# Chunked attention and a gated feed-forward block: a written table of the operations' order in place of a scheduler run at build time, and a third slot for keys

## The chip, the cores and the metric

The kernel runs on one core of a Trainium2 chip. The metric is the device time of one execution in microseconds (us); lower is better.

## What is computed

Four sequences of 768 positions go through attention with 8 heads of 64, and then through a feed-forward block (512 to 1024 and back) with a gate. All is float32; the block's weights come as float64 words. The reference, cut to its core:

```python
for c in range(S // 32):                        # 24 chunks of queries
    l, r = max(0, 32*c - 16), min(S, 32*c + 40) # keys: 16 to the left, 8 to the right
    k_full = concat([mem_k, k[:, :, l:r]])      # and 8 memory keys; v_full likewise
    scores = (q[:, :, 32*c:32*c+32] @ k_full.T) / sqrt(64)
    out[:, :, 32*c:32*c+32] = softmax(scores) @ v_full
x = out as (4, 768, 512)
h = maximum(x @ w_in, 0)
conv = sum(conv_w[j] * h[:, j-1 shifted] for j in 0..2)   # along the positions
result = (h * sigmoid(conv)) @ w_out
```

## The kernel before, in words

The attention is cut into 32 operations, numbered n = 0 to 31: four for each half of a batch's positions (two heads each). Each loads a query tile (384 KB), a key tile (252 KB) and a value tile (384 KB), and then goes through scores (TensorE, L526, 24 matmuls in the 64-row tiled form), their maximum (L535), exponential, sum and division on VectorE, ScalarE and GpSimd (L540 to L572), a transposition, the product with the values (L632, 24 tiled matmuls), and a split of the result into a high and a low part (L635, L638), because the feed-forward products are made of three matmuls each, high by high, high by low and low by high. The transposition goes one of two ways, by the letter in `TURN`: "P" is three matmuls on TensorE (L585) and two copies on ScalarE (L592); "B" is a VectorE transpose (L603), a store to DRAM (L610) and two loads back (L615).

The feed-forward block works by batch: for each of eight slices of 128 hidden features and each half of the positions four steps of three matmuls (L655), then a ReLU; then the gate: a first tap on ScalarE (L681) or VectorE (L685), two more on VectorE (L690), the sigmoid (L693), the product of gate and h on VectorE or GpSimd (L697, letter in `MULT`), and a split into high and low (L702, L705, letter in `LO`). The second product (L718) has six tiles of 128 positions for each batch, eight steps of three matmuls each, a copy (L730) and a store (L734). Weights come in 16 pieces of 512 KB; `from_f64` makes a high and a low part of each, in one of several ways by the letters in `W_IN` and `W_OUT` (R and S with GpSimd's help, M on VectorE, C with ScalarE and GpSimd; a small letter puts one more instruction on GpSimd).

Nothing is issued as the program text stands. Every operation is first put into a `Plan`, with its engine, an assumed cost, a due time out of the table `DUE`, and the tiles it reads and writes; a tile belongs to a pool of slots (`u` 32, `w` 8, `k` 2, `w64` 4 and others). `Plan.run` then plays a simulated timeline, always issues the operation that can start first, by due time among equals, gives tiles their slots, and so fixes the order of the instructions on each engine and in SyncE's queue, through which all DMAs go. On the chip each engine and the queue work in that order, with semaphores between them; a load whose slot isn't free yet holds up every DMA behind it in the queue.

Of the kernel before, what the change touches and what calls it, by code (L numbers as in the profile page):

```python
# [21 lines left out]
NG = NC // 4  # L22
# [7 lines left out]
W_IN, W_OUT, W_CONV = "RMRRCSmr", "MMsScMRC", "M"  # L30
TAP = "AAAAAAVAAVAAAAAAAAVAAVAAAVVAVVAA"
MULT = "VVVGGGVVVGVVGGGGVVGVVGVGGVVGVVVV"
LO = "GVGVVVGGGVVVVVVGGVVVVGVGVGGGGVGG"
SOFT = "VVVVAVAVVVVVVAVAAVAAVVVVAAVAAVVV"
NORM = "GGVVGVGVVGGVGVVGVVVGVGGGVVVGGVGG"
KEEP = "KKKKKNNKKKKKKKKKNKKNNKKNKKNKKNNN"
TURN = "PPPPPPPPBPPBBBBPBBBBPBBBBBBBBBBP"

NU, NW, NK, NE, NA, N64, ND = 32, 8, 2, 3, 2, 4, 4

DUE = {
    "s": [
        -1747.4, -1723.11, -1347.22, -2305.8, -515.97, -91.42, -519.99, -74.77, -3.93, -23.08, 192.31, 394.01, 594.69,
        739.5, 627.96, 843.01, 980.41, 1080.29, 1036.96, 1102.97, 1195.06, 1154.32, 1725.81, 1459.86, 1808.08, 1825.19,
        2056.74, 2405.75, 3024.16, 4272.87, 4420.77, 5096.5,
    ],
    "x": [
        91.99, -984.01, 194.09, 284.75, 339.58, 92.3, 474.48, 424.73, 617.31, 732.06, 742.88, 570.24, 740.55, 840.07,
        827.86, 798.03, 1011.48, 1314.01, 881.59, 1429.56, 1647.93, 1828.11, 1861.16, 1847.69, 1461.7, 1929.84, 2133.48,
        3255.82, 4126.36, 2450.86, 3882.79, 4443.02,  # L50
    ],
    "z": [
        -497.25, -1022.37, -802.58, -289.23, -254.62, -1989.87, -103.33, -205.74, 288.57, -38.79, 65.72, -185.05, 538.06,
        626.96, 491.31, 95.49, 812.34, 1202.49, 806.09, 775.96, 1402.03, 493.56, 2113.26, 1301.38, 1166.49, 986.07, 5915.43,
        5883.56, 6010.45, 4393.97, 4802.83, 4849.77,
    ],
    "t": [
        403.22, 353.24, 332.59, 206.21, -905.28, 65.06, 534.99, 549.9, 636.01, 49.69, 400.09, 693.94, 550.92, 538.53,
        817.29, -606.94, 1153.58, 1304.96, 1055.69, 1495.28, 928.66, 1223.65, 1604.09, 1933.16, 2927.48, 2953.06, 1576.53,
        1798.48, 3734.97, 3794.57, 3033.27, 474.2,  # L60
    ],
    "p": [
        -1059.09, -645.56, -1491.31, -515.31, -415.67, -370.98, -140.64, 75.41, 192.02, 185.23, 433.84, -1978.48, 1014.73,
        818.34, 1439.11, 913.87, 1051.08, 995.86, 2163.84, 1264.46, 2048.92, 3116.62, 1998.39, 3357.56, 4793.09, 4879.62,
        5091.42, 5234.16, 5814.05, 3832.44, 3305.69, 5616.03,
    ],
    "b": [
        1312.85, 933.59, 2887.81, 2282, 2349.62, -94.87, -335.28, 131.64, 364.48, 4687.61, 404.65, 402.37, 633.73, 488.76,
        947.78, 1079.68, 1364.67, 1388.86, 1126.48, 1474.55, 2587.02, 2225.91, 2240.2, 2275.95, 3047.5, 2282.08, 3131.22,
        4577.91, 4647.89, 3535.82, 4762.4, 4239.27,  # L70
    ],
    "v": [
        -1982.49, -1932.67, 479.47, 2099.28, -381.54, 965.03, 1258.45, 1250.02, -432.28, -1997.79, -75.7, -2213.02, -1631,
        -2645.37, 986.28, 303.05, 412.98, -1904.27, -1882.24, 2067.69, 2187.15, -661.87, -294.37, 1472.37, 994.33, 1203.8,
        156.84, 1188.6, 1838.38, 2565.39, 914.94, 1193.87,
    ],
    "y": [
        686.52, 535.63, -757.65, 213.4, -1131.77, 3664.3, 1180.6, 1187.05, -1996.08, -2069.13, -2391.68, -2255.33, 2252.87,
        2426.18, 2577.94, 1767.37, 2904.92, 268.81, 740.16, 1370.82, 3119.59, 4087.13, 1289.4, -2124.16, 1248.74, 1110.03,
        1261.16, -2264.79, 1018.78, -1817, 1016.52, -1388.46,  # L80
    ],
    "rt": [
        -1339.84, -1295.03, -1210.04, -1161.56, -1063.49, -177.47, 139.89, 230.96, 672.21, 615.52, 786.3, 834.64, -1154.66,
        417.82, 1248.11, 1230.62, 1355.39, 689.91, 1375.92, 1505.3, 1500.35, 1002.59, 1206.38, 1555.86, 1459.78, 398.77,
        389.95, 108.41, 927.28, 4860.95, 971.48, 4419.35,
    ],
    "ra": [
        -1586.58, -1104.67, -1041.09, -453.16, 117.35, -211.33, 212.08, 400.73, 726.13, 738.27, 457.13, 809.63, 898.1,
        967.26, 1085.69, 1239.43, 1248.14, 1233.78, 1319.34, 1383.33, 1597.97, 1679.03, 1957.13, 1876.57, 2224.33, 2130.08,
        2332.43, 2747.52, 3912.08, 3522.04, 4787.82, 4516.19,  # L90
    ],
    "lqk": [
        -2184.6, -1037.97, -1000.09, -680.53, -139.13, 73.02, 9.72, 175.02, 258.51, 342.33, 449.15, 439.23, 466.03, 491.4,
        545.13, 557.81, 552.07, 861.22, 717.22, 715.38, 1018.29, 958.68, 1171, 1221.92, 1665.34, 1562.88, 2097.11, 2021.43,
        2134.67, 2357.47, 2162.54, 2666.46,
    ],
    "lv": [
        -405, -703.08, -137.92, -291.15, 263.38, -552.48, -43.43, 410.07, 488.26, 420.11, 499.94, 90.47, 329.01, 690.21,
        724.31, 834.94, 878.3, 921.12, 936.89, 1051.99, 1375.12, 1236.9, 1356.07, 1509.97, 2132.94, 1944.15, 2135.58,
        2125.46, 3089.84, 3488.81, 4358.76, 2957.63,  # L100
    ],
# [6 lines left out]
    ],  # L108
    "ie": [
        105.95, 80.37, -13.89, -54.84, -45.59, -62.67, -107.56, -422.53,  # L110
    ],
    "gate": [
        -10.06, 2306.12, 5455.64, 5546.3, 158.99, 87.7, 1943.75, 1265.91, 1243.7, -452.88, -451.4, -54.24, -87.23, 118.85,
        -111.53, 553.42, 2290.11, -1048.39, 636.65, 531.99, 5015.97, 1531.62, 774.64, 69.66, 1868.09, 1198.4, 5259.66,
        885.34, 2417.49, 2125.3, 1868.5, 383.67,
    ],
    "split": [
        -355.58, -406.33, 3625.04, 679.92, 2594.31, 1824.34, 1652.02, 1654.83, 1888.18, 1132.05, -930.3, 1494.36, 2476.58,
        2202.13, 2602.5, 2706, 2712.83, 1677.79, 2754.72, -288.56, 1962.08, 1890.86, 2314.55, 3843.58, 1376.46, 1681.41,
        1387.06, 3909.1, 1846.4, 2902.43, 1768.28, 2587.34,  # L120
    ],
    "out": [
        1863.21, 1377.79, 2057.4, 1214.28, 1650.53, 2020.46, 3647.4, 2153.83, 4216.03, 3201.8, 4228.87, 4287.47, 4393.4,
        4637, 4588.06, 5409.11, 5397.43, 3850.7, 7778.7, 4801.5, 5550.03, 5548.13, 6410.98, 6455.76,
    ],
    "os": [
        113.08, 152.59, 297.73, 105.3, 90.85, 113.99, -208.31, 155.03, 465.83, 433.18, 174.61, 290.41, 562.87, 319.82,
        430.89, 424.06, 421.99, 719.96, 269.33, 1108.12, 397.72, 748.36, 448.96, 3168.08,
    ],
    "ux": [  # L130
        553.64, 555.79, 372.67, 300.19, 395.15, 317.35, -2521.52, 117.95, 176.19, -298.7, 891.09, 384.34, 1075.63, -234.06,
        318.46, 37.52, -21.55, -6.71, 1098.98, 1151.73, 1294.63, 835.63, 1393.5, 1169.49, 1945.66, 2128.89, 2160.19,
        1903.78, 2471.98, 1644.84, 2560.1, 2496.61,
    ],
# [712 lines left out]
```

## Time and profile before

| | |
|---|---|
| median of 3 runs | 365.48 us (365.38 to 366.71) |
| profiled execution | 368.8 us, of which the span from first to last instruction is 367.0 us |
| TensorE busy | 339.7 us (93% of the span), mean granted clock 0.981 |
| VectorE busy | 247.8 us (68%) |
| ScalarE, GpSimd busy | 209.3 us (57%), 112.7 us (31%) |
| DMA | 56.08 MB |

In the views PE is TensorE's matmuls and PEld its weight loads, DVE VectorE, ACT ScalarE, POOL GpSimd, SPq SyncE's queue. "<-" in a group stands between what is written and what is read. Idle time is put down to the engine or DMA that ended it.

### The profile page before, as it was taken

The numbers are of one execution on the slowest core, as the hardware profiler recorded it, in microseconds if no ns is written. First come the engines' busy times: TensorE is split into PE (matmuls) and PEld (weight loads), VectorE is DVE, ScalarE is ACT, GpSimd is POOL, SyncE is SP. The second block draws the span as 40 slices with busy tenths as digits, with TensorE's granted clock in tenths as the row PEclk, the third lists the DMA queues.
The fourth block names the chain that finished last, engine by engine and source line by source line (L and its number), as shares of the span: only waits on it lengthen the run. The fifth ranks groups of instructions, "written<-read, shape, count | busy, mean of one in ns | idle before, by whom it ended". The sixth has DMA issues, their size and how long they took to land.

```text
span 367.0 us, 7407 instructions
## 1 busy us (share of the span) xinstructions
PE 339.7 (93%) x2943; PEld 301.2 (82%) x2943; DVE 247.8 (68%) x427; ACT 209.3 (57%) x382; POOL 112.7 (31%) x118
## 2 busy tenths in 40 slices
PE   1599899999998989999999988999999999999996
PEld 1489789989897979988987867988988888888885
DVE  1988799999987998899998988214736886000000
ACT  2567766898875977757769676224636654121011
POOL 2455534323134144473433122100010628320000
PEclk9969999999998998999999999999999999999999
DMA  7999473348888384653043868403000010111021
GB/s 254 408 397 361 156 272 103 107 148 268 284 253 284 95 283 128 187 188 118 0 139 121 274 220 271 141 33 123 3 29 0 30 58 29 59 57 57 29 88 57
DMA packets 28114, 56.08 MB, mean 153 GB/s; under 512 B 3248, under 2 KB 14896, under 8 KB 28080
## 3 DMA queue, kind: packets, MB, share of 16 engines
q1 hardware_dynamic: 28080, 55.61, 45.3%
q8 instruction: 23, 0.38, 0.4%
q14 instruction: 11, 0.09, 0.1%
HBM read 45.57 MB, written 10.03 MB: 151 GB/s over the span
## 4 chain that ended last, share of the span: by engine, by line
PE 50%; DVE 14%; DMA 11%; ACT 4%; issue 3%; SPq 2%; POOL 1%; POOLq 0%; DVEq 0%; ACTq 0%
PE f L718 29%; PE f L655 16%; DVE w L690 6%; DMA w<-in_q_dram 6%; PE s L526 3%; DMA t_dram<-w 2%; DMA a_d<-t_dram 2%; PE ta L632 2%; DVE u L697 1%; SPq L615 1%; DVE z L567 1%; DMA k<-in_k_dram 1%; DVE e L572 1%; DVE w L603 1%; DVE u L638 1%
## 5 line engine op out<-in xcount | busy, mean ns | idle before, releaser
L655 PE MATMUL f<-u,w_in_hi 128*128 128x384 f32 x512 | 141.7, 347 | 0.7 <-DVE u L638 0.7
L718 PE MATMUL f<-w_out_hi,u 128*128 128x512 f32 (+1 forms) x400 | 125.6, 388 | 1.1 <-ACT u L669 1.1
L655 PEld LDWEIGHTS f<-u,w_in_hi 128*128 128x128 f32 x512 | 94.8, 191 | 3.8 <-DVE u L638 2.0
L718 PEld LDWEIGHTS f<-w_out_hi,u 128*128 128x128 f32 x400 | 74.0, 188 | 17.9 <-ACT u L669 1.5
L655 PE MATMUL f<-u,w_in_lo 128*128 128x384 f32 x256 | 87.4, 341 | 0.1
L690 DVE SCALAR_TENSOR_TENSOR w<-u,cw,w 128x768 f32<-128x768 f32 x64 | 73.2, 1166 | 6.3 <-ACT w L681 6.0
L718 PE MATMUL f<-w_out_lo,u 128*128 128x512 f32 (+1 forms) x200 | 77.1, 385 | 0.0
L669 ACT ACTIVATE u<-f 128x384 f32<-128x384 f32 x64 | 30.9, 493 | 36.8 <-PE f L655 27.4
L655 PEld LDWEIGHTS f<-u,w_in_lo 128*128 128x128 f32 x256 | 49.1, 192 | 0.9 <-POOL u L668 0.4
L730 ACT COPY w_top<-f 128x512 f32<-128x512 f32 (+1 forms) x25 | 14.1, 573 | 59.8 <-PE f L718 59.1
L718 PEld LDWEIGHTS f<-w_out_lo,u 128*128 128x128 f32 x200 | 37.6, 188 | 7.5 <-POOL w_out_lo L481 0.4
L632 PE MATMUL ta<-a_d,w 128*64 128x64 f32 x768 | 29.4, 230 | 6.6 <-DMA a_d<-t_dram 3.3
L572 POOL TENSOR_TENSOR e<-e,z 128x384 f32<-128x384 f32 x16 | 16.8, 1047 | 61.2 <-DVE z L569 43.8
L632 PEld LDWEIGHTS ta<-a_d,w 128*64 128x64 f32 x768 | 26.1, 143 | 11.1 <-issue 6.7
L697 POOL TENSOR_TENSOR u<-w,u 128x768 f32<-128x768 f32 x11 | 18.5, 1683 | 52.6 <-ACT w L693 52.6
L693 ACT ACTIVATE w<-w 128x768 f32<-128x768 f32 x32 | 26.7, 845 | 11.3 <-DVE w L690 11.0
L705 POOL TENSOR_TENSOR u<-u,u 128x768 fp32r<-128x768 f32 x9 | 17.9, 1990 | 36.5 <-ACT u L702 36.5
L535 DVE TENSOR_REDUCE top<-s 128x6 f32<-128x384 f32 x32 | 17.4, 546 | 16.2 <-PE s L526 16.0
L526 PEld LDWEIGHTS s<-k,w 128*64 128x64 f32 x672 | 22.6, 142 | 6.7 <-issue 3.5
L526 PE MATMUL s<-k,w 128*64 128x64 f32 x672 | 25.3, 229 | 2.8 <-DMA w<-in_q_dram 1.4
L705 DVE TENSOR_TENSOR u<-u,u 128x768 fp32r<-128x768 f32 x13 | 17.8, 1377 | 13.2 <-ACT u L702 10.5
L681 ACT ACTIVATE w<-u,cw 128x768 f32<-128x768 f32 x24 | 22.3, 936 | 1.4 <-DVE u L705 0.6
(65 smaller groups left out, 373.8 us busy)
## 6 DMA issues: line engine op xcount, KB each, us to landing
w<-in_v_dram SPq DMA_DIRECT2D x32, 384.0 KB, 4.8
w<-in_q_dram SPq DMA_DIRECT2D x28, 384.0 KB, 4.5
k<-in_k_dram SPq DMA_DIRECT2D x28, 252.0 KB, 4.2
out_dram<-w_top SPq DMA_DIRECT2D x23, 256.0 KB, 2.0
w<-in_w_in_dram SPq DMA_DIRECT2D x8, 512.0 KB, 7.3
w<-in_w_out_dram SPq DMA_DIRECT2D x8, 512.0 KB, 4.4
t_dram<-w SPq DMA_DIRECT2D x19, 192.0 KB, 2.2
a_d<-t_dram SPq DMA_DIRECT2D x38, 96.0 KB, 3.5
```

Source lines behind the costliest of these rows:

```text
L526: nc.tensor.matmul(s.t[j * D : (j + 1) * D, o : o + KW], lhsT=q_[:, c], rhs=k_t.t[:, c * STEP : c * STEP + KW], start=True, stop=True,)
L535: lambda: V.tensor_reduce(out=pairs(top.t), in_=s_(), axis=AX.X, op=ALU.max), (s,), (top,),
L572: lambda: (V if norm == "V" else G).tensor_tensor(out=keys(e), in0=keys(e), in1=pairs(z.t).unsqueeze(3).broadcast_to([P, NG, 2, KW]), op=A ...
L632: nc.tensor.matmul(y, lhsT=v_[:, g, u, h], rhs=a_d.t[:, :, o], start=True, stop=True)
L655: nc.tensor.matmul(f.t[:, :TW], lhsT=w_in_p[c][:, fc, cc], rhs=x.t[:, a * TW : (a + 1) * TW], start=(cc == 0 and i == 0), stop=(cc == NCC ...
L669: A.activation(h.t[:, o : o + TW], f.t[:, :TW], AF.Relu)
L681: plan.op("A", act(S, ptr=1), due, lambda: A.activation(c.t, at(0), AF.Copy, scale=w[0]), H, (c,))
L690: lambda j=j: V.scalar_tensor_tensor(out=c.t, in0=at(j), scalar=w[j], in1=c.t, op0=ALU.mult, op1=ALU.add),
L693: plan.op("A", act(S), due, lambda: A.activation(c.t, c.t, AF.Sigmoid), (c,), (c,), table="sigmoid")
L697: lambda: (V if mult == "V" else G).tensor_tensor(out=y_(), in0=c.t, in1=at(1), op=ALU.mult), (c, h), (y,), shared=True,
L705: lambda: (V if lo == "V" else G).tensor_tensor(out=g_lo(), in0=y_(), in1=g_hi().bitcast(F32), op=ALU.subtract),
L718: nc.tensor.matmul(ps.t[:, :n], lhsT=gs[b, fc][a].t[:, tt * P : (tt + 1) * P], rhs=w_out_p[c][:, fc, o : o + n], start=(fc == 0 and i == 0 ...
```

## The change

`Plan.run` no longer simulates. It walks a table `ORDER` of 1529 numbers, which are the operations' places in the program text, issues them in that order and hands out slots in the order in which they were given back. The table was searched for under transfer times and a clock that were varied. The due times are gone. The key pool gets a third slot; a new table `HOME` puts six of the 32 value tiles into the pool `w64` instead of `w`. The letters are new: thirteen "P" in `TURN` become seventeen, thirteen "G" in `MULT` become twenty-three, and the kinds of the weights change. In the table the first DMA is the first piece of `w_in`; the first query and key tiles follow it.

```diff
-W_IN, W_OUT, W_CONV = "RMRRCSmr", "MMsScMRC", "M"
-MULT = "VVVGGGVVVGVVGGGGVVGVVGVGGVVGVVVV"
-TURN = "PPPPPPPPBPPBBBBPBBBBPBBBBBBBBBBP"
-NU, NW, NK, NE, NA, N64, ND = 32, 8, 2, 3, 2, 4, 4
-DUE = {
...
+W_IN, W_OUT, W_CONV = "SMMSmMCM", "CMMMCMCM", "r"
+MULT = "VGGGGGGVGVGGGGGGVVGVGGGVGVGGVGGG"
+HOME = "wwwwwwwwwwwwwwwwwwwxwwwwwxxxwwxx"
+TURN = "PPPPPPPPBPPBBPBPBPBBPBPBPBBPBBBB"
+NU, NW, NK, NE, NA, N64, ND = 32, 8, 3, 3, 2, 4, 4
+ORDER = [
+    571, 13, 12, 581, 30, 29, 46, 81, 47, 572, 64, 573, 574, 63, 575, 15, 576, 577, 591, 582, 16, 14, 17, 587, 18, 583, 601,
...
     def run(self):
...
+        idle = {k: deque(v) for k, v in self.pools.items()}
+        done = set()
+        for i in ORDER:
+            do, after, tiles = self.ops[i]
+            assert after <= done
             for x in tiles:
                 if x.slot is None:
+                    x.slot = idle[x.pool].popleft()
+                    x.t = x.slot(x.dtype) if callable(x.slot) else x.slot
+            do()
+            done.add(i)
+            for x in tiles:
                 x.left -= 1
                 if not x.left:
+                    idle[x.pool].append(x.slot)
...
-        v_t = Tile("w")
+        v_t = Tile("w" if HOME[n] == "w" else "w64")
+        v_ = lambda: v_t.t if HOME[n] == "w" else v_t.t.rearrange("p n w -> p (n w)")[:, :S].bitcast(F32)
...
-    nc = _bacc.Bacc("TRN2", target_bir_lowering=False, num_devices=1, dynamic_dma_scratch_size=2048)
+    nc = _bacc.Bacc("TRN2", target_bir_lowering=False, num_devices=1, dynamic_dma_scratch_size=1024)
```

The letters of `TAP`, `LO`, `SOFT`, `NORM` and `KEEP` change too; on VectorE they come to two first taps more and one division less, and the small letters to a few GpSimd instructions.

## Rows read from the trace of the kernel before

**Rows 1.** The page, its first two parts: busy time by engine, and VectorE's tenths

```profile
PE 339.7 (93%) x2943; PEld 301.2 (82%) x2943; DVE 247.8 (68%) x427; ACT 209.3 (57%) x382; POOL 112.7 (31%) x118
DVE  1988799999987998899998988214736886000000
```

**Rows 2.** Busy time in four stages: length, five engines with instructions, granted clock, DMA share, GB/s

```profile
0.00:9.18 9.18, 1.55 (x24) 1.39 (x24) 1.34 (x3) 2.73 (x4) 2.26 (x14) 1.00 0.77 254
0.00:170.00 170.00, 149.71 (x1712) 138.02 (x1712) 146.98 (x299) 120.64 (x232) 67.98 (x85) 0.96 0.69 232
170.00:229.00 59.00, 55.35 (x483) 47.48 (x484) 54.80 (x79) 42.64 (x77) 20.43 (x14) 1.00 0.50 160
229.00:363.40 134.40, 134.40 (x750) 115.66 (x748) 46.00 (x51) 45.33 (x73) 24.25 (x20) 1.00 0.15 52
```

**Rows 3.** TensorE's timeline: start, length, instructions, and in brackets what it idled for

```profile
4.56 1.55 PE L526 MATMUL s<-u,u 128*64 128x64 f32 x24 [4.56 <-DMA u<-in_k_dram]
112.07 0.92 PE L632 MATMUL ta<-a_d,w 128*64 128x64 f32 x24 [1.44 <-DMA w<-in_v_dram]
136.92 0.92 PE L632 MATMUL ta<-a_d,w 128*64 128x64 f32 x24 [1.72 <-DMA a_d<-t_dram]
170.02 0.62 PE L655 MATMUL f<-u,w_in_hi 128*128 128x384 f32 x2 [0.28 <-DVE u L638]
215.31 0.92 PE L632 MATMUL ta<-a_d,w 128*64 128x64 f32 x24 [1.25 <-DMA a_d<-t_dram]
225.37 0.92 PE L526 MATMUL s<-k,w 128*64 128x64 f32 x24 [0.79 <-DMA w<-in_q_dram]
```

**Rows 4.** VectorE's timeline, the idle stretches that the text speaks of

```profile
6.14 0.56 DVE L535 TENSOR_REDUCE top<-s 128x6 f32<-128x384 f32 x1 [6.14 <-PE s L526]
114.61 0.56 DVE L535 TENSOR_REDUCE top<-s 128x6 f32<-128x384 f32 x1 [1.53 <-PE s L526]
144.64 0.56 DVE L535 TENSOR_REDUCE top<-s 128x6 f32<-128x384 f32 x1 [0.98 <-PE s L526]
```

**Rows 5.** The chain that ended last, in order of time: start, length, engine, tile, line

```profile
226.29 0.70 PE ta L632 x24
236.96 4.20 PE f L655 x24
249.68 0.89 PE f L718 x3
252.69 0.33 PE ta L585 x3
277.80 85.50 PE f L718 x390
```

**Rows 6.** Groups by line: count | busy us, mean ns | idle before them

```profile
L421 ACT ACTIVATE w_top<-w 128x512 f32<-128x512 f32 (+1 forms) x17 | 11.1, 652 | 11.4 <-DMA w<-in_w_in_dram 5.7 <-DMA w<-in_w_out_dram 5.5
L690 DVE SCALAR_TENSOR_TENSOR w<-u,cw,w 128x768 f32<-128x768 f32 x64 | 73.2, 1166 | 6.3 <-ACT w L681 6.0
L446 DVE TENSOR_SCALAR w<-w 128x512 uint32<-128x512 uint32 (+1 forms) x9 | 3.8, 437 | 0.5 <-DMA w<-in_w_out_dram 0.5
L451 DVE SCALAR_TENSOR_TENSOR w<-w 128x512 uint32<-128x512 uint32 (+1 forms) x9 | 5.6, 629 | 0.0
L603 DVE STREAM_TRANSPOSE w<-e 128x384 f32<-128x384 f32 x19 | 10.5, 564 | 0.1
```

**Rows 7.** Line 697 alone: duration ns min/median/max, first and last start

```profile
L697 POOL TENSOR_TENSOR u<-w,u x11: 1545/1547/2196, 67.4 to 298.8; 128x768 f32<-128x768 f32 x11
L697 DVE TENSOR_TENSOR u<-w,u x11: 945/948/2096, 67.7 to 302.5; 128x768 f32<-128x768 f32 x11
```

**Rows 8.** Line 690 alone, the same columns

```profile
L690 DVE SCALAR_TENSOR_TENSOR w<-u,cw,w x64: 976/1011/2630, 62.3 to 299.4; 128x768 f32<-128x768 f32 x64
```

**Rows 9.** DMA issues by line: count, KB each, median us to landing

```profile
w<-in_v_dram SPq DMA_DIRECT2D x32, 384.0 KB, 4.8
```

**Rows 10.** SyncE's queue: what its DMA issues waited for (us in total, times, longest)

```profile
SPq L406 <- PE s L526: 33.6, 18, 6.3
```

More of the change, by code (lines that the diff above doesn't have):

```diff
@@ L1 @@
-from collections import defaultdict
+from collections import defaultdict, deque
 from contextlib import ExitStack
@@ L182, in pool, with op @@
         self.pools[name] = slots
-    def op(self, eng, cost, due, do, r=(), w=(), shared=False, table=None, mode=None, late=70, gap=380, less=None):
+    def op(self, eng, cost, do, r=(), w=(), shared=False, table=None, mode=None, late=70, gap=380, less=None):
         after = set()
@@ L206, in op @@
             x.left += 1
-            x.due = due if x.due is None else x.due
-        less = LESS.get(eng, 0) if less is None else less
-        self.ops.append((eng, cost, due, do, after - {i}, tiles, shared, table, mode, late, gap, less))
-        return i
+        self.ops.append((do, after - {i}, tiles))
     def over(self, k):
@@ L219, in run @@
     def run(self):
-        ops = self.ops
-        n = len(ops)
-        users = [[] for _ in range(n)]
-        need = [0] * n
-        for i, o in enumerate(ops):
-            need[i] = len(o[4])
-            for a in o[4]:
-                users[a].append(i)
-        ready = [0.0] * n
-        cand = defaultdict(list)
-        for i in range(n):
-            if not need[i]:
-                cand[ops[i][0]].append(i)
-        free, shared_free, queue_free = defaultdict(float, DMA=FIRST), 0.0, 0.0
@@ L302, in run @@
+        assert sorted(ORDER) == list(range(len(self.ops)))
+        idle = {k: deque(v) for k, v in self.pools.items()}
[3 more added lines that the diff above has]
+            assert after <= done
             for x in tiles:
                 if x.slot is None:
-                    x.slot = min(idle[x.pool])
-                    idle[x.pool].remove(x.slot)
-                    x.slot = x.slot[1]
-                    slot = self.pools[x.pool][x.slot]
@@ L308, in run @@
-                    x.t = slot(x.dtype) if callable(slot) else slot
-                    queue[x.pool].remove(x)
+                    x.slot = idle[x.pool].popleft()
[3 more added lines that the diff above has]
+            for x in tiles:
                 x.left -= 1
-                last_use[x] = max(last_use.get(x, 0), end + late)
                 if not x.left:
-                    idle[x.pool].append((last_use[x] + 70, x.slot))
@@ L314, in run @@
-            do()
-            self.times.append((t, end, e, i))
-            for u in users[i]:
-                ready[u] = max(ready[u], end + (late if ops[u][0] != e or e == "DMA" else 0) + (WAIT if ops[u][0] == "DMA" != e else 0))
-                need[u] -= 1
-                if not need[u]:
-                    cand[ops[u][0]].append(u)
-        return max(x[1] for x in self.times)
-CHANGE = {(None, "whole"): 0, (None, "tiled"): 0, ("whole", "tiled"): 95, ("tiled", "whole"): 245}
-FIRST, BEGIN, LAND, WARM = 720.0, 900.0, 1400.0, 3400.0
+                    idle[x.pool].append(x.slot)
@@ L405, in load, with from_f64 @@
             size *= x
-        plan.op("DMA", size * 4 / RATE, due, lambda: nc.sync.dma_start(out=dst(), in_=src), w=w)
-    def from_f64(src, hi, lo, key, n, kind, due, first):
+        plan.op("DMA", size * 4 / RATE, lambda: nc.sync.dma_start(out=dst(), in_=src), w=w)
+    def from_f64(src, hi, lo, key, n, kind):
         w = Tile("w64")
@@ L585, in turn @@
                     nc.tensor.transpose(out=t.t[:, g * P : (g + 1) * P], in_=e.t[:, g, 1 : 2 * KW + 1], identity=ident)
-            plan.op("PE", 327, turn_due, turn, (e,), (t,), mode="whole", late=250)
+            plan.op("PE", 327, turn, (e,), (t,), mode="whole", late=250)
             for p in range(2):
@@ L595, in place @@
                     )
-                plan.op("A", 480, place_due, place, (t,), ((a_d, p),), less=-10)
+                plan.op("A", 480, place, (t,), ((a_d, p),), less=-10)
         else:
@@ L631, in values @@
                             o, y = h * 6 + 2 * g + u, a.t[r, g * P : (g + 1) * P].rearrange("p (j u q) -> p u j q", j=2, u=2)[:, u]
-                        nc.tensor.matmul(y, lhsT=v_[:, g, u, h], rhs=a_d.t[:, :, o], start=True, stop=True)
-        plan.op("PE", 700, sum_due, values, (v_t, (a_d, 0), (a_d, 1)), (a,), mode="tiled", late=250)
-        plan.op("A", act(TW, True), due, lambda: A.copy(out=x.t[:, :TW], in_=a.t[:, :TW]), (a,), ((x, 0),))
+                        nc.tensor.matmul(y, lhsT=v_g[:, g, u, h], rhs=a_d.t[:, :, o], start=True, stop=True)
+        plan.op("PE", 700, values, (v_t, (a_d, 0), (a_d, 1)), (a,), mode="tiled", late=250)
+        plan.op("A", act(TW, True), lambda: A.copy(out=x.t[:, :TW], in_=a.t[:, :TW]), (a,), ((x, 0),))
         plan.op(
-            "V", vec(TW), due,
+            "V", vec(TW),
             lambda: V.tensor_tensor(
@@ L709, in ffn_out @@
     def ffn_out(b, tt, parts=1):
-        start, each = DUE["out"][6 * b + tt], DUE["os"][6 * b + tt]
         n = DM // parts
@@ L732, in ffn_out @@
             plan.op(
-                "DMA", P * n * 4 / RATE, last,
+                "DMA", P * n * 4 / RATE,
                 lambda o_sb=o_sb, o=o: nc.sync.dma_start(
```

292 lines of the change are left out of this document (51 added, 241 removed), and 73 rows, old and new, of tables (DUE, ORDER).

## The prediction

> **What bounds the kernel now.** I read the page first. TensorE is busy 93% of the span, so only about 27 us of its idle time can be won, and VectorE, at 68% on the whole, shows eights and nines from the second slice to the twenty-third and almost nothing in the last five [rows 1]. The busy time by stage makes two halves of that. Up to 229 us both engines are nearly full; from 229 to 363.4 us TensorE is busy for 134.40 of 134.40 us at full clock while VectorE works for 46.0 us [rows 2]. So the last stage is TensorE's alone, no order can shorten it, and the question is when TensorE gets clear of VectorE. TensorE's timeline shows where it stood still before: 4.56 us for the first keys, then 1.44 us for values, 1.72 and 1.25 us for the probabilities' way through DRAM, 0.79 us for a query load, and at 170.02 us it stood once for a VectorE result [rows 3]. VectorE began only at 6.14 us, behind the first scores, and stood 1.53 and 0.98 us for scores that TensorE gave late, each behind one of TensorE's two long DMA waits [rows 3, 4]. Up to 170 us VectorE was busy for 146.98 us, so it idled for 23.0 us, 7.84 of them in the first 9.18 us [rows 2].
>
> In short: the end is (VectorE's work ahead of the tightest point) + (VectorE's idle time up to there) + (TensorE's work behind it) + (TensorE's idle time behind it).
>
> **The change part by part.** Prices on TensorE are those of the dense stretches of the chain: 0.70 us for a block of scores or values, 4.20 / 24 x 3 = 0.525 us for a step of the first product, 85.50 us for 390 matmuls (24 of them half as wide), so 0.68 us for a step of the second, 0.33 us for a turn, and about 0.2 us for a change between tiled and whole matmuls (0.89 against 0.68) [rows 5].
>
> *The flags.* Thirteen operations' turns were on TensorE (P) and seventeen will be: +4 x 0.33 = 1.3 us. I counted the changes between tiled and whole in both orders: 52 before, 54 after, +0.4 us. TensorE gets 1.7 us more to do; at least 4 x 0.175 = 0.7 us (a turn moves no fewer columns than one matmul of the first product). Each turn moved also takes one store and two loads off SyncE's queue, twelve DMAs in all. On VectorE ten products of line 697 go to GpSimd: -10 x 0.95 us [rows 7]. The weights' kinds bring fifteen instructions from GpSimd back to it: seven with one input at about 0.44 and eight with two at about 0.63, +8.1 us [rows 6]. Four transposes fewer, -4 x 0.56 = -2.3 us [rows 6], stand against two first taps more at no more than 1.17 each, by the row of line 690. VectorE's total hardly moves (about -1.4 us), and GpSimd and ScalarE, at 31% and 57% [rows 1], have room for theirs. The ten products cost GpSimd 1.55 us each instead of 0.95 [rows 7]; what is late by 0.6 us is the split that follows, and the second product, which needs it, comes long behind.
>
> *Line 697 and the port.* Line 690 takes 1011 ns in the median and 1166 in the mean over 64, line 697 on VectorE 948 ns in the median and 2096 at most [rows 6, 7, 8]; so some of these instructions are held up, by 0.16 us each on average. The ten moved products may so cost VectorE ten times that, 1.6 us, of which the fifteen weight instructions that leave GpSimd give about as much back. I take nothing; the bounds are nothing and a hold of a whole 1.55 us each (a rival below). The Trainium skill ("SBUF — State Buffer", Who interferes with whom) says that a VectorE instruction with two SBUF inputs and a GpSimd instruction that reads SBUF exclude each other for the whole instruction. Taken at its word for each of the ten, moving them off VectorE wins nothing; the maxima of rows 7 and 8 agree with it, the medians show that most instructions meet no such hold.
>
> *The order.* I numbered the operations as the program makes them and walked both orders, adding to each engine's queue the price of each instruction (its group's mean in the view by line; VectorE's scaled by 0.925, since its means overlap and add up to 267.8 us where 247.8 are busy [rows 1]). For each TensorE step this gives the VectorE work that must be over before it, less the TensorE work ahead of it. Before, the largest difference is 17.8 us, at the first product of batch 2, second half (154.3 against 136.6 of 321.8): the place where TensorE stood for VectorE at 170.02 us [rows 3]. As a check: 170.0 + (321.8 - 136.6) + 3.65 us of TensorE's idle time up to 229 [rows 2] = 358.9 where the chain's last matmul ends at 363.3 [rows 5]; the method is 1.2% short, so I use it for differences alone. After, it is 18.1 us at the turn of operation 22 (148.6 against 130.5), and again 17.4 us at that of operation 24 (192.4 against 174.9). The tight point hardly moves: +0.3 us.
>
> *The loads.* What does move is how early the DMAs stand. Between a load and its first use the old order has on average 4.9 us of TensorE work for queries and 11.9 for values, and for five query and five value loads none at all; the new one has 10.4 and 17.1, and beyond the first five operations never under 5.5. From the last load of the DRAM round trip to the values block it has 5.2 us or more where the old one has often 2.6 to 3.6. A value load takes 4.8 us from issue to landing [rows 9]: the old leads are often below that, the new ones above. The third key slot and the six value tiles moved to another pool make room for this: 18 loads waited 33.6 us for scores to give a slot back [rows 10]. What these leads can win is VectorE's 1.53 + 0.98 us ahead of the tight point and TensorE's 1.25 + 0.79 us behind it [rows 3, 4], 4.55 us. TensorE's own 1.44 and 1.72 us are not added, since VectorE was the later one there. I take two thirds, 3.0 us, as some other operand is late next; bounds 0 and 4.55, and beyond that the clock: 0.96 granted on average over 149.71 busy us up to 170 [rows 2] means some 12 us at 1.2 GHz, 6 us lost, a part of it behind TensorE's two long waits.
>
> *The start.* The new order issues the first weight load ahead of the first query and keys. The first pair, 636 KB, let TensorE begin at 4.56 us [rows 3], so 512 KB issued at the same moment land no later; with 0.65 us on ScalarE [rows 6] VectorE can begin near 4.9 (an estimate, from a landing at 4.2) instead of at 6.14 us [rows 4] and has five instructions (some 2.6 us) to do until the first scores come, about 1.5 us later than now. Before, it did 1.34 us of work by 9.18 us [rows 2]; now I expect 3.7, as about 0.6 us stay idle: -2.4 us. Bounds: nothing (the scores' delay eats it) and -2.9 (no idle time behind 4.9).
>
> **Sum:** +1.7 (TensorE) + 0.3 (tight point) - 3.0 (loads) - 2.4 (start) = -3.4 us. The profiled execution took 368.8 us, 1.8 of them outside its span, and would so come to 365.4; it was 3.3 us above the median of the runs, 365.48, from which the same sum gives 362.1 us.
>
> **The rivals.** *The waits only move.* Slots, not issue times, hold the loads, or an operand from ScalarE is late in their place, and the loads win nothing: 365.48 + 2.0 - 2.4 = 365.1 us. For it: VectorE stays full in both orders, and the tight point stays. *The order wins more.* All 4.55 us of waits go, with 3 of the 6 us at half clock, and the start wins 2.9: 365.48 + 2.0 - 4.55 - 3 - 2.9 = 357.0 us. For it speak the leads; against it that VectorE would have to be busy without a break. *SyncE's queue blocks (slower).* The table's order is also the queue's: where a slot comes free late, every load behind it waits, and the queue waited up to 6.3 us for one slot [rows 10]. One such wait that reaches TensorE, with some 2 us at half clock behind it, gives 362.1 + 8.3 = 370.4 us; it decides from a lead that is overrun by more than 5.5 us. Against it speak the longer leads. *The port (slower).* Each moved product holds VectorE for 1.55 us. Six of the ten lie in the first three batches, ahead of the later tight point: 362.1 + 6 x 1.55 = 371.4 us. By the Trainium skill's rule named above it would come to this; against it stand the medians of rows 7 and 8.
>
> **How the numbers follow.** The forecast has 0.47, the waits that only move 0.23, more won 0.12, the queue 0.12, the port 0.06. About 0.5%, 1.8 us, is what a measurement can tell here, so faster ends at 363.7 and slower begins at 367.3. Faster is the forecast and more won, less a little of the forecast's upper edge: 0.58; same 0.24; slower the two last: 0.18. The forecast's own range is 359 to 364; to hold eight in ten it reaches to the greater gain on one side, 355.5, and into the slower cases on the other, 368.0.
>
> **What would show it.** Right: VectorE's first instruction near 4.9 us; over 3 us less VectorE idle time up to 170 us; no TensorE wait for a load over 1 us between 30 and 230 us; TensorE without a break from some 3 us earlier than 229; 51 turn matmuls. Wrong: a new wait of over 2 us on TensorE, for a DMA or a copy; a mean of line 690 well above 1166 ns; SyncE standing at a slot while the next load is already needed.

## The result, and the profile after

The changed kernel takes 367.88 us in the median of 20 executions (366.09 to 370.45), the kernel before 365.59 us beside it (362.76 to 368.36, 20): a ratio of 1.0072, 95% interval 1.0044 to 1.0100. It is 0.7%, some 2.6 us, slower, where 362.1 us and a gain were forecast. The two profiled executions stand the other way round (368.8 us before, 366.92 us after), because the one of before is a long one of its kind and the one of after a short one; so sizes are taken from the medians, and the profiles serve to show where the time lies.

The page of the changed kernel, busy time and VectorE's tenths:

```profile
PE 339.9 (93%) x2955; PEld 301.4 (83%) x2955; DVE 252.0 (69%) x429; ACT 210.6 (58%) x387; POOL 104.6 (29%) x114
...
DVE  4999999999999999998999956230444991320000
```

Busy time in the stages of [rows 2] (length, then PE, PEld, DVE, ACT, POOL, granted clock, DMA):

```profile
0.00:9.18 9.18, 1.69 (x27) 1.56 (x29) 4.05 (x8) 2.61 (x3) 3.53 (x15) 1.00 0.78 296
0.00:170.00 170.00, 149.82 (x1721) 138.04 (x1722) 158.15 (x301) 126.14 (x250) 55.24 (x78) 0.99 0.67 232
170.00:229.00 59.00, 58.56 (x507) 50.78 (x505) 51.74 (x83) 40.07 (x67) 24.97 (x15) 1.00 0.43 141
229.00:361.50 132.50, 131.00 (x726) 112.24 (x727) 42.09 (x46) 43.99 (x70) 24.34 (x22) 1.00 0.14 50
```

VectorE's idle time up to 170 us is 170 - 158.15 = 11.9 us, where it was 23.0 [rows 2]; the forecast counted on at most 4.9 of that (2.4 at the start, 2.5 at the loads). By 9.18 us it has done 4.05 us of work in this execution (1.34 before, 3.7 forecast), and its first instruction starts at 4.96 us (4.9 forecast), in VectorE's timeline:

```profile
4.96 0.43 DVE L280 TENSOR_SCALAR w_top<-w_top 128x512 f32<-128x512 f32 x1 [4.96 <-ACT w_top L276]
```

TensorE's timeline shows what it stood for (four of its idle stretches, in brackets):

```profile
6.14 1.55 PE L381 MATMUL s<-u,u 128*64 128x64 f32 x24 [6.14 <-DMA u<-in_q_dram]
...
147.94 0.55 PE L439 MATMUL ta<-ident,e 128*128 128x128 f32 x3 [2.14 <-DVE e L427]
...
161.32 0.62 PE L508 MATMUL f<-u,w_in_hi 128*128 128x384 f32 x2 [0.80 <-DVE u L492]
...
230.50 0.44 PE L508 MATMUL f<-u,w_in_hi 128*128 128x384 f32 x1 [1.59 <-ACT u L522]
```

No wait for a load is left between 30 and 230 us; those of [rows 3] are gone, as forecast. In their place stand waits for VectorE's results, 2.14 us at the turn of operation 20 and 0.80 us at 161.32 us, just ahead of the turn of operation 22, where the walk had its tight point (18.1 us). TensorE's last break ends at 230.50 us, where the forecast had it without a break from some 3 us ahead of 229. The idle time that the forecast meant to win is gone, and yet TensorE is no further: up to 170 us it has been busy for 149.82 us, as before (149.71, at a granted clock of 0.96 instead of 0.99). VectorE idles 11 us less and is busy 11 us more.

The groups by line, and line 543 alone as in [rows 8], show a part of what it is busy with (L543 is line 690 of before, L550 line 697):

```profile
L543 DVE SCALAR_TENSOR_TENSOR w<-u,cw,w 128x768 f32<-128x768 f32 x64 | 78.1, 1231 | 4.4 <-ACT w L534 3.7
...
L543 DVE SCALAR_TENSOR_TENSOR w<-u,cw,w x64: 979/1014/2601, 58.4 to 299.5; 128x768 f32<-128x768 f32 x64
...
L550 POOL TENSOR_TENSOR u<-w,u 128x768 f32<-128x768 f32 x16 | 28.9, 1810 | 41.5 <-ACT w L546 41.5
...
L550 POOL TENSOR_TENSOR w<-w,u 128x768 f32<-128x768 f32 x7 | 13.4, 1915 | 11.4 <-ACT w L546 10.5 <-POOL u L521 0.9
```

The two taps on VectorE take 1231 ns in the mean, 1166 before [rows 6]; there are 64 in both. Their median is 1014 ns, as good as the 1011 of [rows 8]: most run undisturbed, and some are more than twice as long. VectorE's total rose by 4.2 us, where a fall of 1.4 was counted. A stretch of the two timelines, VectorE first and then GpSimd, shows how:

```profile
123.30 1.01 DVE L543 SCALAR_TENSOR_TENSOR w<-u,cw,w 128x768 f32<-128x768 f32 x1
...
125.10 2.31 DVE L543 SCALAR_TENSOR_TENSOR w<-u,cw,w 128x768 f32<-128x768 f32 x1
...
128.27 3.22 DVE L543 SCALAR_TENSOR_TENSOR w<-u,cw,w 128x768 f32<-128x768 f32 x2
131.41 0.54 DVE L492 TENSOR_TENSOR u<-ta,u 128x384 fp32r<-128x384 f32 x1
...
132.34 3.23 DVE L543 SCALAR_TENSOR_TENSOR w<-u,cw,w 128x768 f32<-128x768 f32 x2
```

```profile
125.05 1.55 POOL L550 TENSOR_TENSOR u<-w,u 128x768 f32<-128x768 f32 x1 [5.15 <-ACT w L546]
128.36 2.31 POOL L550 TENSOR_TENSOR u<-w,u 128x768 f32<-128x768 f32 x1 [1.77 <-ACT w L546]
132.45 2.31 POOL L550 TENSOR_TENSOR u<-w,u 128x768 f32<-128x768 f32 x1 [1.77 <-ACT w L546]
```

The tap at 123.30 us runs alone, 1.01 us. The one at 125.10 us begins just behind a GpSimd product that started at 125.05 and takes 2.31 us. At 128.27 us it is the other way: the product starts 0.09 us behind the first of two taps and is stretched from 1.55 to 2.31 us, and the second tap waits for it, 3.22 us for the two. They run one after the other, on two engines.

### The profile page after: what moved, and what is told of

It is laid out like the page before. It is cut to its first block, busy times and chain, and to the rows that moved or that the text cites. A ratio compares the mean times of both kernels' runs of the same rounds, so it can differ in the third digit from the quotient of the medians.

```text
span 365.1 us, 7418 instructions
## 1 busy us (share of the span) xinstructions
PE 339.9 (93%) x2955; PEld 301.4 (83%) x2955; DVE 252.0 (69%) x429; ACT 210.6 (58%) x387; POOL 104.6 (29%) x114
## 4 chain that ended last, share of the span: by engine, by line
PE 41%; DVE 21%; ACT 5%; issue 2%; DMA 1%; POOL 1%; SPq 0%; DVEq 0%; ACTq 0%; POOLq 0%
PE f L569 29%; PE f L508 10%; DVE w L543 9%; DVE w_top L293 2%; PE ta L486 1%; DVE e L427 1%; DVE z L422 1%; DVE u L492 1%; DVE top L390 1%; DVE u L557 1%; DMA w<-in_q_dram 1%; ACT u L522 1%; ACT e L413 1%; DVE w L457 1%; DVE e L395 1%
## 5 line engine op out<-in xcount | busy, mean ns | idle before, releaser
L508 PE MATMUL f<-u,w_in_hi 128*128 128x384 f32 x512 | 143.8, 347 | 6.2 <-ACT u L522 3.8
L508 PEld LDWEIGHTS f<-u,w_in_hi 128*128 128x128 f32 x512 | 94.6, 190 | 10.4 <-ACT u L522 5.1
L543 DVE SCALAR_TENSOR_TENSOR w<-u,cw,w 128x768 f32<-128x768 f32 x64 | 78.1, 1231 | 4.4 <-ACT w L534 3.7
L550 POOL TENSOR_TENSOR u<-w,u 128x768 f32<-128x768 f32 x16 | 28.9, 1810 | 41.5 <-ACT w L546 41.5
L492 DVE TENSOR_TENSOR u<-ta,u 128x384 fp32r<-128x384 f32 x32 | 17.5, 548 | 12.8 <-ACT u L489 12.7
L557 DVE TENSOR_TENSOR u<-u,u 128x768 fp32r<-128x768 f32 x9 | 9.4, 1058 | 20.7 <-PE f L569 10.0
L557 POOL TENSOR_TENSOR u<-u,u 128x768 fp32r<-128x768 f32 x11 | 21.5, 1955 | 5.4 <-ACT u L554 3.5
## 6 DMA issues: line engine op xcount, KB each, us to landing
k<-in_k_dram SPq DMA_DIRECT2D x28, 252.0 KB, 4.5
```

Source lines behind the costliest of these rows:

```text
L492: lambda: V.tensor_tensor(out=x.t[:, TW:S], in0=a.t[:, :TW], in1=x.t[:, :TW].bitcast(F32), op=ALU.subtract), (a, (x, 0)), ((x, 1),),
L508: nc.tensor.matmul(f.t[:, :TW], lhsT=w_in_p[c][:, fc, cc], rhs=x.t[:, a * TW : (a + 1) * TW], start=(cc == 0 and i == 0), stop=(cc == NCC ...
L543: lambda j=j: V.scalar_tensor_tensor(out=c.t, in0=at(j), scalar=w[j], in1=c.t, op0=ALU.mult, op1=ALU.add),
L550: lambda: (V if mult == "V" else G).tensor_tensor(out=y_(), in0=c.t, in1=at(1), op=ALU.mult), (c, h), (y,), shared=True,
L557: lambda: (V if lo == "V" else G).tensor_tensor(out=g_lo(), in0=y_(), in1=g_hi().bitcast(F32), op=ALU.subtract),
```

## The experiments

Two theories stood against each other. **P**: a product on GpSimd holds up VectorE's instructions with two SBUF inputs, so that the ten moved products freed nothing. **Q**: VectorE pays for the instructions that it is given, and holds are rare. Later **W** (the weight instructions brought to VectorE), **E** and **V** (what the early loads are worth) and **T** (the product is late on the slower engine) were added. Ratios are to the kernel before, run on the same chip, with 95% intervals; it is the ratios that are compared, since the kernel before itself had medians of 365.56 to 366.62 us beside these runs.

**The old order in a table.** The walker, `ORDER` taken from the old planner, old letters and slots.

> The kernel before with its own order, letters and slots counts, but issued from a table by the new walker (slots handed out in the order of their return). Both theories: the order on each engine is that of before, so 365.6 us within 1 us; if it is slower by over 1 us, the handing out of slots costs something by itself.

Measured 365.91 us, ratio 1.0013 (0.9981 to 1.0045): no change from the walker itself. Its profiled execution (span 364.6 us) had the full clock, and its page serves as a second one of before, here with the busy time up to 165 us (the changed kernel's below it):

```profile
PE 337.6 (93%) x2943; PEld 297.7 (82%) x2943; DVE 248.0 (68%) x427; ACT 209.1 (57%) x382; POOL 113.6 (31%) x118
...
0.00:165.00 165.00, 144.97 (x1675) 132.58 (x1676) 144.72 (x293) 118.72 (x229) 68.50 (x84) 1.00 0.69 235
...
0.00:165.00 165.00, 144.82 (x1662) 133.28 (x1664) 154.82 (x295) 123.76 (x245) 55.24 (x78) 0.99 0.67 232
```

VectorE's 144.72 and 154.82 us are 10.1 us apart, for 293 and 295 instructions.

**The products' letters, either way.**

```diff
 # before_mult_new: the old order in a table
-MULT = "VVVGGGVVVGVVGGGGVVGVVGVGGVVGVVVV"
+MULT = "VGGGGGGVGVGGGGGGVVGVGGGVGVGGVGGG"
 # mult_old: the changed kernel, the reverse
```

> The kernel before, from a table, with one edit: the MULT letters of the changed kernel, so that ten products go from VectorE to GpSimd (five of them in batches 0 and 1). Theory P (a product on GpSimd holds up VectorE's two-input instructions of line 690 by some 1.2 us each time that they meet): the mean of those instructions rises from 1166 to 1230 ns or more, and the time is not lower, 365 to 369 us. Theory Q (VectorE's own work ahead of the tight point counts, holds are rare): VectorE has 5 x 0.95 us less ahead of it, the mean stays under 1190 ns, 361 to 363 us.

> The changed kernel with one edit: the MULT letters of before, so that ten products go back to VectorE. Theory P: the mean of the two-input instruction of the taps falls from 1231 to under 1170 ns, VectorE's busy time grows by less than 4 us although it gets ten instructions of 0.95 us, and the time is 364 to 367 us, below the changed kernel's 367.9. Theory Q: VectorE has 4.8 us more ahead of the tight point, 371 to 373 us.

The first gave 370.28 us, ratio 1.0130 (1.0094 to 1.0165): ten products moved off VectorE make the old kernel 4.7 us slower. The taps' mean rose to 1242 ns, and VectorE's busy time fell from 248.0 to 243.9 us, 0.41 us a product and not 0.95. The order was not made for these letters, so some of the 4.7 us may be lateness, which this run doesn't separate. The second gave 366.78 us, ratio 1.0032 (1.0013 to 1.0051), 1.5 us below the changed kernel's ratio; the taps' mean was 1190 ns, above P's 1170, and VectorE's busy time rose by 1.2 us for ten instructions of 0.95. Its page, and its busy time up to 165 us, by which five of the ten have run:

```profile
PE 338.5 (93%) x2955; PEld 298.1 (82%) x2955; DVE 253.2 (69%) x439; ACT 210.5 (58%) x387; POOL 85.7 (24%) x104
...
0.00:165.00 165.00, 143.85 (x1687) 130.67 (x1689) 154.78 (x300) 123.90 (x246) 45.38 (x73) 1.00 0.68 233
```

Five instructions more take VectorE no longer: 154.78 against 154.82 us. Q is out in both. P's direction holds; its sizes hold roughly (370.28 us is above its 369, and 1190 ns above its 1170).

**More products on VectorE.** `MULT` of the changed kernel with "V" for batches 0 and 1; for all; for batches 0 to 2.

> The changed kernel with the thirteen GpSimd products of batches 0 and 1 on VectorE. With one column each the 23 products freed VectorE of 19.2 us of held time, 0.84 us each, so theory P (a product on GpSimd costs VectorE in held instructions about what it saves): VectorE's busy time up to 165 us stays at 153 to 156 us, the mean of the taps' instruction falls below 1150 ns, and the time is 364 to 367 us, lower than the changed kernel's 367.9, since the product itself is there sooner. Theory Q (VectorE pays for each instruction that it gets): 13 x 0.95 = 12.4 us more ahead of the tight point, 375 us or more.

> The changed kernel with all 32 products on VectorE. Theory P: 23 x 0.95 - 19.2 = 2.7 us more VectorE time in all, most of it behind the tight point; mean of the taps' instruction below 1080 ns; 364 to 368 us. Theory Q: 375 us or more.

> The changed kernel with the products of batches 0 to 2 on VectorE and those of batch 3, where VectorE is no longer full, as in the changed kernel. Theory P: about what all on VectorE gave, 366.5 to 368.5 us, since a product costs VectorE the same on either engine. A version below before's 365.6 would need VectorE to gain from the six late ones: 364 to 365 us.

368.55 us, 1.0073 (1.0038 to 1.0107); 368.14 us, 1.0065 (1.0037 to 1.0093); 368.34 us, 1.0076 (1.0046 to 1.0106). All stand where the changed kernel stands; the first is above P's 364 to 367 us, the second 0.1 us above its 368, and Q's 375 us is out. With all 23 brought over VectorE has 22 us of instructions more, and its busy time is 253.1 us instead of 252.0:

```profile
PE 338.8 (93%) x2955; PEld 299.8 (82%) x2955; DVE 253.1 (69%) x452; ACT 210.8 (58%) x387; POOL 64.5 (18%) x91
```

So in this order VectorE pays the same for a product on either engine, and none of the five splits that were run beats the kernel before.

**The products made small.** GpSimd's products compute one column of 768 and leave out the rest.

```diff
-lambda: (V if mult == "V" else G).tensor_tensor(out=y_(), in0=c.t, in1=at(1), op=ALU.mult)
+lambda: V.tensor_tensor(out=y_(), in0=c.t, in1=at(1), op=ALU.mult) if mult == "V" else
+    G.tensor_tensor(out=y_()[:, 0:1], in0=c.t[:, 0:1], in1=at(1)[:, 0:1], op=ALU.mult)
```

> The changed kernel, but each of the 23 products on GpSimd computes one column of 768 and leaves out the rest; the order and all waits stay. Theory P: the mean of the two-input instruction of the taps falls from 1231 to under 1100 ns, VectorE is busy for 8 us less or more, and the time falls to 358 to 362 us. Theory Q: GpSimd's products lie beside the path and hold up little, so the time stays at 366 to 368 us.

> The kernel before, from a table, with its 13 GpSimd products computing one column of 768 and leaving out the rest; order and waits stay. In the changed kernel the same edit took 12 us off (355.95 against 367.9). Theory P (held instructions ate the change's gain): here it takes off 6 us or less, 359.5 to 362.5 us, so that without products on GpSimd the changed kernel is the faster one by 3.5 us or more, near what was forecast for it. Theory W (holds cost both the same; the weights or the order ate the gain): 10 us or more come off, 353 to 356 us.

The changed kernel falls to 355.95 us, 0.9737 (0.9698 to 0.9776), 3.3% below itself, and VectorE's busy time from 252.0 to 232.8 us, though none of its own instructions was touched:

```profile
PE 336.1 (95%) x2955; PEld 299.8 (85%) x2955; DVE 232.8 (66%) x429; ACT 209.8 (59%) x387; POOL 72.5 (20%) x114
```

The old one falls to 362.37 us, 0.9875 (0.9838 to 0.9912). Without GpSimd's products the changed kernel is the faster by 0.9737 / 0.9875 = 0.986, 5.1 us. The two edits take away both the hold and the lateness.

**Lateness kept, reading taken away.** The product's column, then two memsets of the other 767, which read nothing; the product is left out.

```diff
+G.tensor_tensor(out=y_()[:, 0:1], in0=c.t[:, 0:1], in1=at(1)[:, 0:1], op=ALU.mult)
+for _ in range(2):
+    G.memset(y_()[:, 1:], 0.5)
```

> The changed kernel with each of its 23 products on GpSimd replaced by one column of the product and two memsets of the other 767 (some 0.74 us each by the memsets at the kernel's start), which only write: GpSimd is busy about as long and the result is there about as late, but nothing is read from SBUF for 1.5 us; the product itself is left out. Theory P (it is the reading that holds VectorE): the taps' mean falls to 1032 to 1080 ns and the time to 356 to 360 us, as with one column alone. Theory T (it is the product's lateness behind a slower engine): taps' mean may fall, but the time stays at 364 to 368 us.

> The kernel before, from a table, with its 13 GpSimd products replaced in the same way (product left out). Theory P: 361 to 363 us, as with one column alone (362.4). Theory T: 364.5 to 366.5 us.

In the changed kernel GpSimd is as busy as before the edit (104.7 us against 104.6), each memset takes 0.74 us, and yet the taps' mean is 1031 ns and VectorE's busy time 234.1 us; the page, and groups by line on VectorE and GpSimd:

```profile
PE 335.7 (94%) x2955; PEld 298.5 (84%) x2955; DVE 234.1 (66%) x429; ACT 209.9 (59%) x387; POOL 104.7 (29%) x160
```

```profile
L543 DVE SCALAR_TENSOR_TENSOR w<-u,cw,w 128x768 f32<-128x768 f32 x64 | 65.3, 1031 | 4.4 <-ACT w L534 3.7
```

```profile
L554 POOL MEMSET u<- 128x767 f32 x32 | 23.7, 740 | 0.9
...
L554 POOL MEMSET w<- 128x767 f32 x14 | 10.5, 749 | 0.4
```

The time is 358.01 us, 0.9786 (0.9751 to 0.9821). Against the changed kernel's 1.0072 that is 0.9786 / 1.0072 = 0.972, 10.4 us, of the 12.2 that the small products won: the reading costs 10.4, the lateness some 2, which is no more than the two intervals leave open. In the old kernel the same edit takes VectorE's busy time from 248.0 to 239.4 us,

```profile
PE 337.1 (93%) x2943; PEld 298.1 (82%) x2943; DVE 239.4 (66%) x427; ACT 209.2 (58%) x382; POOL 115.9 (32%) x144
```

but the time only to 365.05 us, 0.9987 (0.9961 to 1.0013): no difference that can be measured. There VectorE's busy time falls by 8.6 us and the end hardly moves, so that its holds lay in time that it would have idled; what small products won there was lateness. T holds for the old kernel, P for the changed one. Without the hold the changed kernel stands at 0.9786 / 0.9987 = 0.980 of the old one.

**The loads.** 56 query, key and value loads of operations 5 to 31 go back in `ORDER` to the old order's distance from their use (the lead, in TensorE work).

```diff
-ORDER = [571, 13, 12, 581, ...]   # mean lead 10.4 us for queries, 17.1 for values
+ORDER = [571, 13, 12, 581, ...]   # 56 loads later: 4.5 and 8.4 (the old order: 4.9 and 11.9)
```

A load goes back only where the old distance was the shorter one, so that on the whole the loads stand later than in either order.

> The changed kernel with 56 query, key and value loads of operations 5 to 31 put back in the table to the old order's distance from their use (in TensorE work between load and use). Theory E (the early loads won what was forecast, 3.0 us or more, and something else ate it): TensorE waits for loads again, 370 to 374 us. Theory V (VectorE is full up to the tight point, so the loads' time won nothing that lasts): the time stays within 1.5 us of the changed kernel's, 366.5 to 369.4 us, though the trace shows waits for loads.

380.23 us, 1.0391 (1.0341 to 1.0441): 12 us are lost, more than E gave, and V is out. TensorE's timeline shows two waits for query loads, longer than the 0.79 us of [rows 3]:

```profile
115.99 1.55 PE L312 MATMUL s<-k,w 128*64 128x64 f32 x24 [3.07 <-DMA w<-in_q_dram]
...
233.02 1.55 PE L312 MATMUL s<-k,w 128*64 128x64 f32 x24 [4.66 <-DMA w<-in_q_dram]
```

This order needs its early loads. What they are worth against the old order isn't shown: this run's value leads, 8.4 us, are shorter than the old order's 11.9, so its 12 us would overstate them.

**The start.** The first query and keys ahead of the first weights in the changed kernel; in the old order the reverse, with the first piece's four VectorE instructions in front.

```diff
-    571, 13, 12, 581, ...
+    13, 12, 571, 581, ...
```

> The changed kernel with the first query and key tiles loaded ahead of the first weight piece, as before; VectorE's order stays, with the weight piece first. If the early weights win what was forecast (2.4 us of VectorE work by 9.18 us), VectorE starts some 1.5 us later and the time rises to 369 to 370.5 us. If the start wins nothing that lasts: 367 to 368.7 us.

> The kernel before, from a table, with the changed kernel's start alone: the first weight piece is loaded ahead of the first query and key tiles, and its first four VectorE instructions stand ahead of the first scores' maximum. If the start wins what was forecast, VectorE has done 2 us or more of extra work by 9.18 us, and the time is 363 to 364.5 us, below before's 365.6; if the later scores eat it, 365 to 367.5 us.

369.93 us, 1.0093 (1.0057 to 1.0128), and 365.66 us, 0.9987 (0.9962 to 1.0012). The first median lies in the range for a start that won what was forecast, but the kernel before was slow beside it too (366.62 us): by the ratios it is 0.8 us above the changed kernel, give or take some 1.7 us, so neither nothing nor 2.4 us is excluded. The second is no different from before, but it doesn't test the early work, which didn't come about: by 9.18 us VectorE has done 1.99 us, against 1.71 in the table form of before, and not 2 us more (TensorE's first scores had to wait for their keys until 7.58 us, until 4.93 there). Busy time of the second in 9.18 us, of the first in 9.18 and 27.5 us and from there to 165, then of the changed kernel in the last two:

```profile
0.00:9.18 9.18, 1.55 (x24) 1.39 (x24) 1.99 (x5) 2.81 (x4) 3.29 (x15) 1.00 0.75 257
```

```profile
0.00:9.18 9.18, 1.55 (x24) 1.39 (x24) 1.21 (x3) 2.22 (x3) 2.26 (x14) 1.00 0.79 248
0.00:27.50 27.50, 12.71 (x205) 10.60 (x206) 18.90 (x43) 12.69 (x30) 6.43 (x18) 1.00 0.90 319
27.50:165.00 137.50, 126.52 (x1434) 116.98 (x1433) 132.36 (x247) 108.36 (x211) 49.69 (x60) 0.99 0.64 212
```

```profile
0.00:27.50 27.50, 16.89 (x214) 14.88 (x215) 21.24 (x49) 13.78 (x33) 7.50 (x19) 1.00 0.95 366
27.50:165.00 137.50, 127.93 (x1450) 118.41 (x1450) 133.58 (x247) 109.98 (x213) 47.74 (x60) 0.99 0.61 206
```

With the old start VectorE is 2.8 us of work behind the changed kernel at 9.18 us, 2.3 at 27.5 and 3.6 at 165; in these two executions none of it is made good up to there. From 27.5 to 165 us VectorE is busy for 133.58 of 137.50 us in the changed kernel, and in the old one, from the table, for

```profile
27.50:165.00 137.50, 128.96 (x1483) 119.19 (x1482) 126.11 (x250) 105.26 (x205) 56.88 (x62) 1.00 0.64 211
```

**The weights.** Eight pieces of the old kernel in kinds C and M; twelve, three and six pieces of the changed kernel in kinds S and R, with operations that would come too early put back behind what they need.

```diff
 # before_weights_new (and N64 = 5, NU = 31)
-W_IN, W_OUT = "RMRRCSmr", "MMsScMRC"
+W_IN, W_OUT = "CMCCCMmc", "MMmMcMCC"
 # weights_s, weights_out_some, weights_some (and with the old MULT)
-W_IN, W_OUT = "SMMSmMCM", "CMMMCMCM"
+W_IN, W_OUT = "SSSSsSRS", "CSSSRMRS"
+W_IN, W_OUT = "SMMSmMCM", "CSMSCMCS"
+W_IN, W_OUT = "SMMSsSRM", "CSMSCMCS"
```

> The kernel before, from a table, in its order, with eight weight pieces made in the changed kernel's manner (kinds C and M for R and S, so 16 instructions more on VectorE, some 9 us, and 16 fewer on GpSimd; a fifth slot for w64 and one u slot less, which the order doesn't use). Theory W: VectorE is 92% busy between 27.5 and 165 us already, so that most of the 9 us lands on the path: 369 to 374 us. Theory P: the GpSimd instructions that go away stop holding VectorE, and the idle time takes up the rest: 364 to 367 us.

> The changed kernel with twelve weight pieces made with GpSimd's help again (kinds S and R for M and C; operations that come too early in the table are put back behind what they need): VectorE has 24 instructions less, some 13 us, GpSimd 24 more. Theory W (the weight instructions brought to VectorE are what filled it ahead of the tight point): VectorE is busy for 10 us less or more, 360 to 364 us. Theory P: GpSimd's two-input instructions on 512 columns hold VectorE as the products do, so at least half of the 13 us comes back as longer instructions, and the time is 366 to 372 us.

> The changed kernel with three pieces of w_out (1, 3, 7) made in kind S instead of M: 6 VectorE instructions less (3.3 us), 6 GpSimd instructions more. Theory W (the weights' instructions fill VectorE also in the changed kernel's own order): 365 to 367 us, below the changed kernel's 367.9. Theory P (what leaves VectorE comes back as held instructions): 367 to 369 us.

> As the run above, and three pieces of w_in (4, 5, 6) in kinds S and R too: 12 VectorE instructions less (6.6 us), 12 GpSimd instructions more. Theory W: 362 to 365 us. Theory P: 367 to 370 us.

> As the run above, with the MULT letters of before as well (ten products back on VectorE, which alone gave 366.8). Theory W: the two gains add, 361 to 364 us, below both kernels. Theory P: 366 to 369 us.

The old kernel goes to 370.93 us, 1.0134 (1.0097 to 1.0171), in W's range and above P's, but not for W's reason: its VectorE has 16 instructions more and is no busier in total,

```profile
PE 338.1 (92%) x2943; PEld 298.6 (81%) x2943; DVE 247.6 (67%) x443; ACT 209.6 (57%) x382; POOL 89.1 (24%) x102
```

247.6 against 248.0 us, while GpSimd's busy time falls by 24.5 us. In the changed kernel undoing the kinds makes it slower each time: 393.41 us, 1.0745 (1.0704 to 1.0786); 373.11 us, 1.0197 (1.0148 to 1.0245); 378.63 us, 1.0358 (1.0315 to 1.0400); with the old products too 377.32 us, 1.0340 (1.0291 to 1.0390). All four are above the ranges of both theories. With three pieces VectorE's total falls by 2.9 us to 249.1, nearly the 3.3 that W counts, with six only to 248.9; but results come late: TensorE's timeline of the one with three pieces shows waits that the changed kernel doesn't have,

```profile
166.97 2.83 PE L417 MATMUL ta<-a_d,w 128*64 128x64 f32 x48 [2.71 <-ACT a_d L377]
...
192.88 0.50 PE L500 MATMUL f<-w_out_lo,u 128*128 128x512 f32 x1 [0.85 <-POOL w_out_lo L267]
```

one of them for a weight's low part made on GpSimd. W is out as a forecast of the time: less work on VectorE did not make this order faster. Putting other kinds under an order that was made without them cost 4 us or more on both sides; what the kinds are worth with an order of their own stays open.

## Why the prediction was wrong

**TensorE's extra work** (+1.7 us): 51 turn matmuls are there. TensorE's busy time, at full clock in both, is 337.6 us in the table form of before and 338.5 in the changed kernel with the old `MULT`, +0.9 (its own 339.9 us were taken at a granted clock of 0.995). Right within a microsecond.

**The loads** (-3.0 us): the mechanism was right as far as the trace shows it: the waits for loads of [rows 3] are gone, and with the loads late such waits are back. The size of 3.0 us is neither confirmed nor refuted.

**The start** (-2.4 us): the work done early was right in the profiled execution (4.05 us against 3.7; the other runs with the same start give 2.67 to 3.85). Its worth stays open: the one run that tests it gives 0.8 us with an uncertainty of some 1.7.

**Line 697 and the port** ("On VectorE ten products of line 697 go to GpSimd: -10 x 0.95 us", with the hold "I take nothing"): this is the step that failed. The saving of 9.5 us on VectorE was taken in full and its price at nothing. Measured, the ten products are worth 1.2 us of VectorE's time in the new order (252.0 against 253.2 us with the old letters) and 4.1 in the old one, and nothing at all ahead of 165 us (154.82 against 154.78). VectorE's total came out 5.6 us higher than counted (+4.2 instead of -1.4). As an estimate from the prediction's own terms: six of the ten lie ahead of the later tight point, and without their saving of 6 x 0.95 = 5.7 us its sum of 362.1 becomes 367.8 us, where 367.9 was measured. That it fits so closely may be luck, since the sizes of the loads and the start in that sum are not confirmed.

What eats the saving is the hold. Taking the reading away from the 23 products wins 10.4 us, while for the 13 of the old kernel it wins nothing that can be measured (1.0013 and 0.9987); without the reading in either, the changed kernel would stand 2% below the old one. The rival named for this (the port, 371.4 us, chance 0.06) had the mechanism and was 3.5 us too high: it took 1.55 us for a product's hold, where the memsets in place of 23 products give VectorE 17.9 us back, 0.78 each. In the timeline from 125 to 136 us the product's 1.55 us lie between two taps or ahead of one, and whichever comes second waits. The Trainium skill ("SBUF — State Buffer", Who interferes with whom) has the rule: a VectorE instruction with two SBUF inputs and a GpSimd instruction that reads SBUF exclude each other, one that only writes doesn't disturb. The timeline agrees with the first half, the run with memsets (1031 ns) with the second.

The medians of [rows 7, 8] were read wrongly. They can't price a hold that fewer than half of the instructions meet: the median of the taps is 1014 ns in the changed kernel too, where the mean is 1231, the prediction's own sign of being wrong. And they tell of the old order, where VectorE idled for 23 us, and not of one that leaves it hardly a gap.

**VectorE's work ahead of the tight point** (+0.3 us): the walk used the old kernel's mean durations, so the ten moved products counted as saved. With one mean for each line it could not see that the holds move from behind the tight point to ahead of it. The 32 taps of batches 0 and 1 in the groups by line, up to 170 us before and up to 162.8 us now:

```profile
L690 DVE SCALAR_TENSOR_TENSOR w<-u,cw,w 128x768 f32<-128x768 f32 x32 | 33.5, 1073 | 0.0
...
L543 DVE SCALAR_TENSOR_TENSOR w<-u,cw,w 128x768 f32<-128x768 f32 x32 | 41.0, 1287 | 0.4
```

They are busy for 7.5 us more, ahead of the tight point, while five of the ten products, 4.8 us, have left.

The forecast of which waits would go was right; that waiting for another engine's reads would fill the time won was given a price of zero. Not settled are the shares of the weight kinds, of the loads and of the new start, and why the old order lost 4.7 us to the new letters.

## What to carry to other kernels

An elementwise instruction with two SBUF inputs that moves from VectorE to GpSimd can free VectorE of nothing while VectorE has two-input instructions of its own to run: here 23 products cost VectorE as much on GpSimd as on itself (252.0 and 253.1 us), and in the old order ten gave back 0.41 us each instead of 0.95. Such a hold doesn't show as idle time but as longer instructions, so look at the mean and the maximum of a line beside its median, and at both timelines, before the idle time. And when an order closes the gaps of an engine, price its instructions as they run without gaps, not by their means in the old order.

## What the runs showed that was not expected

A memset of 767 columns on GpSimd (0.74 us) running beside the taps leaves them at 1031 ns, while a product of 768 columns that reads (1.55 us alone, 2.31 when it has to wait itself) takes those that it meets to 2.3 us. For each product VectorE was held about as long in both kernels (8.6 us over 13, 17.9 over 23: 0.66 and 0.78 us), but in time the one total was worth no more than 1 us, within the intervals, and the other 10.4: the first disappeared in gaps.
